# Odd heads' scores with swapped token halves, in a recurrent attention with two feed-forward layers on one core

## The chip, the core and the metric

The program runs on one core of a Trainium2 chip: a matrix engine (TensorE, PE), a vector engine (DVE), a scalar engine (ACT), GpSimd (POOL) and SyncE (SP), which issues the DMAs here. Times are microseconds on the device for one execution; lower is better.

## What is computed

An attention with a decaying state, token by token, over 4 batch entries, 8 heads, 768 tokens, 48 columns per head, and behind it two feed-forward layers on 3072 tokens of width 384:

```python
for t in range(S):
    cur = np.einsum('bhd,bhe->bhde', u[None] * kt, vt)
    y[:, :, t] = np.einsum('bhd,bhde->bhe', rt, state + cur)
    state = wt[:, :, :, None] * state + np.einsum('bhd,bhe->bhde', kt, vt)
# x: y with the heads side by side
xn = x / rms * rms_g
x = (silu(xn @ w_gate) * (xn @ w_val)) @ w_out         # d_ff 1536
out = (s * np.maximum(x @ w_in, 0) ** 2 + b) @ w_out2  # d_ff 2048
```

All of it is float32.

## The kernel before

Tokens are cut into 6 chunks of 128. A pair of chunk and batch entry is a block `jb` (24 of them, four to a chunk); `attention(jb, t)` does one. Both feed-forward layers take a chunk at a time, all four batch entries side by side, so that a dense pass on PE streams 512 columns: L646 is the product into the hidden width, L629 to L631 the product out of it (three passes for each of three output tiles, since a number is split into a high and a low part). The attention of a chunk runs while the first layer of the chunk before it is on PE.

Nothing is issued in the order of the code. Each step is handed to a planner (`op`) with a due time `t`, a cost for each engine that can do it, and what it reads and writes. The planner plays the program through with these costs, takes on each engine the ready step that is due first, and writes every engine's instructions in that order. A hundred or so due times are set by hand in a table, by the number of the operation, up to number 921. Waits between engines follow from what is read and written. The planner's costs that the prediction uses, in us: a dense pass 0.226; ACT's copy of one bank 0.19 + 0.65e-3 x 512 = 0.523; a select 0.60; the way from a step's end to a step on another engine 0.20 after PE, 0.15 after ACT and 0.10 after POOL; a DMA issue at least 0.47.

A block from the 13th (`jb` 12) on goes like this. SP loads decays (`w`), `r` and `k` of a block turned so that head columns lie on partitions (even heads on partitions 0 to 47, odd on 64 to 111, four head pairs `h` side by side), the natural `r` and `k` (`n`), and `v` with tokens on partitions. DVE scans the decays into products; `r` and `k` are multiplied with them (DVE or POOL). `k` is turned by a DVE transpose and a round trip through DRAM (`kd`, read back into `raw`, which the code calls TK). Then, on PE:

- **scores** (L404): for each head pair h, token half c0 and parity p, a product of 64 tokens of k with the tokens of r from c0 on. c0 = 0 gives 128 columns, c0 = 64 gives 64, since earlier tokens are masked. Its 64 results land on PSUM partitions c0 to c0 + 63, and its inputs lie on partitions from 64p on, so that each such product takes one of four quarters of the array. p chooses the PSUM bank.
- ACT copies each of the two banks to SBUF (128x512, `AT`), POOL sets what lies on or below the diagonal to zero (L426, affine_select, in place).
- **state** (L445) and **sums** (L454), one step for the planner: r with the carried state, and the masked scores with `v`, 64 output tokens at a time; then the products for the new state (L463), which read `v` and TK.
- DVE adds the term of u, ACT and POOL normalize, DVE transposes the result, and SP writes it to DRAM (`xt`) and, with the chunk's last block, reads it back for the layers.

SP issues its DMAs in the planner's order, each when what it waits for is there.

Of the kernel before, what the change touches and what calls it, by code (L numbers as in the profile page):

```python
# [17 lines left out]
ALU = mybir.AluOpType  # L18
# [4 lines left out]
B, H, S, D = 4, 8, 768, 48  # L23
C = 128
NC = S // C
HP = H // 2
DM = H * D
# [20 lines left out]
W_TINY, W_HUGE = 1.125 * 2.0 ** -15, 1.875 * 2.0 ** 16 - 2.0 ** -7  # L48
FA, HALF = 6, (4, 6)
ATT = 30.0, 6.0, 0.0, 18.0, 20.0, 20.0, 20.0, 0.0  # L50
TD, LATE = 3, 60
ORDER = -200, -190, -170, -160, -180, -150
FIRST_OPS = {
# [19 lines left out]
TURNED, EARLY, NU, NM, NZ, LENT = 12, 12, 4, 4, 8, 6  # L73
# [145 lines left out]
def mm(n, k=1):  # L219
    return k * (0.013 + n / 2400.0)  # L220
# [3 lines left out]
def body(ctx: ExitStack, tc: tile.TileContext, rkw, nat, w1, w2, cst, out):  # L224
    nc = tc.nc
# [5 lines left out]
    def tiles(n, name, shape, dt=F32):  # L231
        return [sb.tile(shape, dt, name=f"{name}{i}") for i in range(n)]
# [15 lines left out]
    OT = tiles(2, "o", [128, NB])  # L248
    IN = tiles(2, "in", [128, RKW])
    VT = tiles(2, "v", [128, H, D])  # L250
    NT, = tiles(1, "n", [128, 2, H, D])
    EB = [[t] for t in tiles(2, "eb", [RW, HP, WL])]
    KT = tiles(1, "kt", [128, HP, RW])
    AT = tiles(3, "a", [128, HP, C])
# [47 lines left out]
    def op(when, engines, fn, reads=(), writes=(), port=True):  # L302
        if planned[0]:
            reads, writes = [alias.get(k, k) for k in reads], [alias.get(k, k) for k in writes]
            plan.add(when, engines, fn, reads, writes, port)
        else:
            fn(next(iter(engines)))

    def dma(when, dst, src, nbytes, reads=(), writes=(), land=0.0):
        op(when, {"sp": max(0.47, nbytes / 350e3 + 0.06) + 0.5 * (when == -300)}, lambda e: nc.sync.dma_start(  # L310
            out=dst, in_=src), reads, writes, land)

    def tt(when, engines, n, dst, a, b, f, reads, writes):
        cost = {"dve": vec2(n), "pool": gps(n)}
        port = not any(k[0] == "ps" for k in reads)
        op(when, {e: cost[e] for e in engines}, lambda e: E[e].tensor_tensor(dst, a, b, f), reads, writes, port)  # L316

    def cp(when, n, dst, src, reads, writes, func=AF.Copy, **kw):
        op(when, {"act": act(n)}, lambda e: nc.scalar.activation(dst, src, func, **kw), reads, writes)  # L319
# [3 lines left out]
    def ring(name, of):  # L323
        rings[name] = rings.get(name, -1) + 1
        return of[rings[name] % len(of)]
# [9 lines left out]
    def attention(jb, t):  # L335
        q, b = jb % 2, jb % B
        AVK = [("av", q, h0) for h0 in range(0, H, 2)]
        ke, re, ne = (DVE, DVE, DVE) if jb < EARLY else (BOTH, BOTH, BOTH)
        last = jb >= NJ - B
        a, v, g, z = IN[q][:RW], VT[q], RG[q], q if jb < NZ else 0  # L340
        n = [RK[z][:, i * DM:(i + 1) * DM].rearrange("p (h d) -> p h d", h=H) for i in range(2)]
        ET, BT, kt, xg = EB[0][z], EB[1][z], KT[z], XG[z]
        ek, bk, nk, tk, xk = ("E", z), ("bk", z), ("n", z), [("kt", z)], ("xg", z)
        turned = jb >= TURNED
        rk = RK[z][:RW, 0:HP * C].rearrange("p (h t) -> p h t", h=HP)
        r = a[:, OR:OK].rearrange("p (h t) -> p h t", h=HP)
        k = a[:, OK:].rearrange("p (h t) -> p h t", h=HP)
        if jb in (TURNED, TURNED + 1):
            op(t - 15, {"pool": 0.5}, lambda e: nc.gpsimd.memset(IN[q][96:128, OK:], 0.0), (), [("k", q)], False)
        tl = [FIRST[jb] + 0.1 * i for i in range(4)] if jb < B else [t - 14 + 0.1 * i for i in range(4)]  # L350
        dma(tl[0], a[:, 0:OR], rkw[jb, :, 0:OR], RW * OR * 4, (), [("w", q)])
        dma(tl[1], a[:, OR:], rkw[jb, :, OR:], RW * 2 * HP * C * 4, (), [("r", q), ("k", q)])
        if jb >= NU:
            dma(tl[2], RK[z], nat[jb, :, DM:], 128 * 2 * DM * 4, (), [nk])
        dma(tl[3], v.rearrange("p h d -> p (h d)"), nat[jb, :, 0:DM], 128 * DM * 4, (), [("v", q)])

        op(t, {"dve": 1.15}, lambda e: nc.vector.tensor_tensor_scan(
            ET.rearrange("p h t -> p (h t)"), a[:, 0:HP * WL], ones.rearrange("p h t -> p (h t)"), 0.0,
# [16 lines left out]
        if turned and not last:  # L375
            tk = [("kt", i) for i in range(4)]
# [3 lines left out]
        sc = [PS[i].rearrange("p (h t) -> p h t", h=HP) for i in i2]  # L380
# [17 lines left out]
        def scores(e):  # L398
            for h in range(HP):
                for c0 in (0, 64) if jb >= B else (0,):  # L400
                    cols = slice(c0, c0 + 64 if jb >= B else C)
                    for p in range(2):
                        rows = slice(64 * p, 64 * p + D)
                        nc.tensor.matmul(sc[p][cols, h, c0:], k[rows, h, cols], r[rows, h, c0:],  # L404
                                         start=True, stop=True, skip_group_check=True)
            if kp is not None:
                for h in range(HP):
                    nc.tensor.transpose(kp[:, h, :], k[:, h, :], ident[:RW, :RW])  # L408
# [11 lines left out]
        A = [ring("a", (0, 1, 2, 3) if jb < NZ else (0, 1, 2)) for p in range(2)]  # L420
        for p in range(2):
            if jb < NM:
                tt(t, DVE, HP * C, AT[A[p]], sc[p], mask, ALU.mult, [("ps", i2[p]), "m"], [("a", A[p])])
                continue
            cp(t, HP * C, AT[A[p]], sc[p], [("ps", i2[p])], [("a", A[p])])
            op(t, {"pool": 0.60}, lambda e, s=A[p]: nc.gpsimd.affine_select(  # L426
                out=AT[s], in_=AT[s], compare_op=ALU.is_gt, fill=0.0, base=0, pattern=[[0, HP], [1, C]],
                channel_multiplier=-1), (), [("a", A[p])])
        if kp is not None:
            cp(t, HP * RW, kt, kp, [("ps", i)], tk)  # L430
        if jb < NU:
# [4 lines left out]
        Y = [PS[i][:, 0:DM].rearrange("p (h d) -> p h d", h=H) for i in (iy * 2)[:2]]  # L436
# [3 lines left out]
        def state(e):  # L440
            for h in range(HP):
                for c0 in (0, 64):
                    for p in range(2):
                        rows = slice(64 * p, 64 * p + D)
                        nc.tensor.matmul(Y[p][c0:c0 + 64, 2 * h + p, :], r[rows, h, c0:c0 + 64], ST[b][rows, h, :],  # L445
                                         start=h == 0, stop=False, skip_group_check=True)

        def sums(e):
            if jb >= B:
                state(e)  # L450
            for j in range(H):
                h, p = divmod(j, 2)
                for c0 in (0, 64):
                    nc.tensor.matmul(Y[p][c0:c0 + 64, j, :], AT[A[p]][:, h, c0:c0 + 64], v[:, j, :],  # L454
                                     start=jb < B and j == 0, stop=j >= H - 2, skip_group_check=True)
            if U is not None and jb >= B:
                news(e)
# [18 lines left out]
        reads = [("a", s) for s in A]  # L476
        if jb < B:
            op(t, {"pe": 1.0}, sums, reads + [("v", q)], [("ps", i)])
            op(t, {"pe": 0.7}, more, AVK + ["cs"], [("ps", i)])
            op(t, {"pe": 0.6}, news, [("v", q)] + tk, [("ps", iu)])  # L480
            ys, yk = PS[i][:, 0:DM], ("ps", i)
        else:
            op(t, {"pe": 1.5 + 0.6 * (not last)}, sums,
               reads + [("r", q), ("v", q), ("st", b)] + tk * (not last),
               [("ps", i) for i in iy] + ([] if last else [("ps", iu)]))
            ys, yk = YS[q], ("ys", q)
            for p in range(2):
                y2, a2, s2 = [x.rearrange("p (h j d) -> p h j d", h=HP, j=2)[:, :, p] for x in (
                    PS[iy[p]][:, 0:DM], AV[q].rearrange("p h d -> p (h d)"), ys)]
                tt(t, DVE, HP * D, s2, y2, a2, ALU.add, [("ps", iy[p])] + AVK, [yk])  # L490
# [5 lines left out]
        if not last:  # L496
            st, pmb = ST[b], PM[q].to_broadcast([RW, HP, D])
# [346 lines left out]
    beg, parts, t = {}, [], T0  # L844
# [7 lines left out]
    for jb in range(NJ):  # L852
        c, b = divmod(jb, B)
        if c == 0:
            t = ready = ORDER[b]
        elif c == 1:
            t = ready = beg[1, 0] - 34 + 9 * b
        elif c == 2:
            t = beg[1, 1] - LAG + 10.5 * b
            ready = max(t, beg[1, 1] + 0.01)  # L860
        else:
            t = beg[c - 1, 0] + b * (F1 * step + ATT[4]) / B - LAG
# [4 lines left out]
    for n, (c, fs) in enumerate(parts):  # L867
# [4 lines left out]
        t = beg[c, int(fs[0] > 0)]  # L872
        for p in part:
            d = (len(fs) * step + ATT[n]) * p[3] / (B * len(fs))
            seq.append((t, d) + p + (p[1] == fs[0], p[1] == fs[-1], int(fs[0] > 0)))
            t += d
    for f in range(F1):
        if f < FA:
            t = ORDER[B + f] if f < 2 else T0 + (f - 2) * 5.5
        else:  # L880
            t = beg[0, 1] + (f - FA - 4) * 5.5
# [7 lines left out]
    last = beg[NC - 1, 0]  # L889
    later(last, hand_over, last)  # L890
    for f in range(F2):
        t = last + min(2 * f // 3 + 3.5, F1 + 0.6 * (f - 15)) * 27 * mm(NB)
        later(t, weights, 1, f, t, slots_of(1, f))
    for c in range(NC):
        t2 = T1 + c * d2
        x = c % 2
        later(t2 - 12, x2_in, t2 - 12, c, x)
        for f in range(F2):
            d, q = d2 / F2, (len(seq) + f) % 2
            for b0, nb in ((0, 2), (2, 2)) if c == NC - 1 and f == F2 - 1 else ((0, B),):  # L900
                t = t2 + (f + b0 / B) * d
# [17 lines left out]
    with tc.If(flag > 0):  # L919
# [11 lines left out]
        w, r, k, kv, sc = (a[:RW] for a in big[:5])  # L931
        uc = PM[0][:, 0, :]
        with tc.For_i(0, B, 1) as b:
            with tc.For_i(0, HP, 1) as h:
                for dst, o, wd in ((w, 0, WL), (r, OR, C), (k, OK, C)):
                    src = rkw[:, :, o:o + HP * wd].rearrange("(c b) p (h t) -> b h p c t", b=B, h=HP)
                    nc.sync.dma_start(out=dst.rearrange("p (c t) -> p c t", c=NC), in_=src[b, h][:, :, wd - C:])
                vs = vn[:, 0:NC * 2 * D].rearrange("p (c m) -> p c m", c=NC)
                nc.sync.dma_start(
                    out=vs, in_=nat[:, :, 0:DM].rearrange("(c b) t (h m) -> b h t c m", b=B, h=HP)[b, h]  # L940
# [28 lines left out]
                for i in range(2):  # L969
                    vec.tensor_copy(vT[:2 * D, i * HC:(i + 1) * HC], ya[i])  # L970
                nc.sync.dma_start(
                    out=xd.rearrange("(h m) c b t -> h b m c t", h=HP)[h, b],
                    in_=vT[:2 * D].rearrange("p (c t) -> p c t", c=NC),
                )
        with tc.For_i(0, NC, 1) as c:
            x = IN[0][:, 0:KD * NB].rearrange("p (k t) -> p k t", k=KD)
# [17 lines left out]
            for ph, nf in ((0, F1), (1, F2)):  # L994
                for f in range(nf):
                    sw = range(3 * (f % 2), 3 * (f % 2) + 3 - ph)
                    weights(ph, f, 0, sw, clamp=True)
                    q, t = f % 2, SG[f % 2]
# [37 lines left out]
```

## Time and profile before

| | us |
|---|---|
| three runs | 967.93, 967.55, 966.31 |
| median | 967.55 |
| profiled execution | 967.64 |
| its span, first to last instruction | 965.9 |

A page of the profile gives, for each engine, its busy time and share of the span, then the busy tenths in 40 slices of 24 us, and the chain of work that ended last, followed back from the last instruction. The views behind it list instructions in order of time, groups of instructions, and waits. The matrix engine's products are pipelined, so they overlap, and a busy time is the union of what ran. A float32 product of the attention shows as two passes.

### The profile page before, as it was taken

What the parts mean: (1) busy time and instruction counts of PE and PEld (TensorE: products, weight loads), DVE (VectorE), ACT (ScalarE), POOL (GpSimd) and SP (SyncE); (2) the same over time, 40 slices, a digit from 0 to 9 for tenths busy, and PEclk for the clock granted to TensorE, in tenths of its full rate; (3) what the DMA queues carried; (4) which work ended last, traced back from release to release, by engine and by line L of the source; (5) the groups of instructions that cost most, each with busy time, mean ns of one, the idle gap of its engine ahead of it and who ended that gap; (6) DMA issues with size and microseconds to landing.
All of it is one profiled execution on the core that took longest, in us unless ns stands there. A gap on an engine that the chain in (4) does not pass through costs nothing.

```text
span 965.9 us, 16522 instructions
## 1 busy us (share of the span) xinstructions
PE 952.9 (99%) x6585; PEld 788.7 (82%) x6589; DVE 635.2 (66%) x1051; ACT 378.8 (39%) x782; POOL 162.6 (17%) x211
## 2 busy tenths in 40 slices
PE   9999999999999999999999999999999999999996
PEld 5898998888888887888888878888888888888885
DVE  8999898547445445532588799987777874433332
ACT  4756545534323332332343353343433433433333
POOL 1212211255433323110025440000000000000000
PEclk9999999999999999999999999999999999999998
DMA  8655554245434443222466465553354530000001
GB/s 259 196 169 158 173 158 140 83 112 149 101 84 118 122 93 95 69 69 61 122 225 206 150 212 178 158 194 113 114 182 132 178 117 1 33 0 1 34 1 36
DMA packets 74422, 115.79 MB, mean 120 GB/s; under 512 B 28384, under 2 KB 48096, under 8 KB 74336
## 3 DMA queue, kind: packets, MB, share of 16 engines
q1 hardware_dynamic: 74336, 114.65, 39.6%
q8 instruction: 53, 0.87, 0.4%
q14 instruction: 33, 0.27, 0.1%
HBM read 99.16 MB, written 15.47 MB: 119 GB/s over the span
## 4 chain that ended last, share of the span: by engine, by line
PE 91%; DVE 5%; DMA 2%; ACT 1%; issue 1%; SPq 0%; POOL 0%; DVEq 0%
PE b L646 48%; PE b L629 12%; PE b L630 11%; PE b L631 11%; PE b L454 2%; PE b L404 2%; PE b L445 1%; DMA raw<-in_w 1%; DMA in<-in_rkw 1%; DVE pat L605 1%; DVE pat L603 1%; PE b L408 0%; PE b L822 0%; PE b L469 0%; DVE pat L599 0%
## 5 line engine op out<-in xcount | busy, mean ns | idle before, releaser
L646 PE MATMUL b<-xh,w 128*128 128x512 f32 (+1 forms) x1566 | 485.2, 374 | 0.9 <-DVE sg L316 0.6
L646 PEld LDWEIGHTS b<-xh,w 128*128 128x128 f32 x1566 | 287.7, 188 | 55.6 <-issue 1.9
L646 PE MATMUL b<-xl,w 128*128 128x512 f32 (+1 forms) x783 | 291.1, 372 | 0.0
L629 PE MATMUL b<-hh,w 128*128 128x512 f32 (+1 forms) x537 | 205.0, 382 | 1.1 <-ACT in L681 0.7
L630 PE MATMUL b<-hl,w 128*128 128x512 f32 (+1 forms) x537 | 202.5, 377 | 1.4 <-DVE hl L316 1.4
L631 PE MATMUL b<-hh,w 128*128 128x512 f32 (+1 forms) x537 | 202.1, 376 | 0.0
L319 ACT ACTIVATE sg<-b 128x512 f32<-128x512 f32 (+1 forms) x179 | 102.6, 573 | 249.1 <-PE b L646 245.0
L646 PEld LDWEIGHTS b<-xl,w 128*128 128x128 f32 x783 | 147.3, 188 | 25.4
L717 DVE SCALAR_TENSOR_TENSOR sg<-sg,cs,b 128x512 f32<-128x512 f32 (+1 forms) x97 | 71.9, 741 | 90.0 <-ACT sg L319 89.8
L630 PEld LDWEIGHTS b<-hl,w 128*128 128x128 f32 x537 | 101.0, 188 | 20.2 <-DVE hl L316 2.5
L629 PEld LDWEIGHTS b<-hh,w 128*128 128x128 f32 x537 | 101.0, 188 | 20.1 <-ACT in L681 0.9
L631 PEld LDWEIGHTS b<-hh,w 128*128 128x128 f32 x537 | 101.0, 188 | 18.5
L720 DVE SCALAR_TENSOR_TENSOR hl<-sg,cs,hh 128x512 fp32r<-128x512 f32 (+1 forms) x97 | 73.0, 753 | 43.4 <-ACT hh L319 43.2
L319 ACT ACTIVATE hh<-sg,cs 128x512 fp32r<-128x512 f32 (+1 forms) x97 | 70.1, 722 | 75.9 <-DVE sg L717 71.4
L319 ACT ACTIVATE hh<-sg 128x512 fp32r<-128x512 f32 (+1 forms) x82 | 47.6, 581 | 114.9 <-DVE sg L316 109.5
L316 DVE TENSOR_TENSOR sg<-b,sg 128x512 f32<-128x512 f32 (+1 forms) x82 | 51.0, 623 | 62.1 <-PE b L646 52.9
L316 DVE TENSOR_TENSOR hl<-sg,hh 128x512 fp32r<-128x512 f32 (+1 forms) x82 | 57.3, 698 | 18.2 <-ACT hh L319 17.5
L620 POOL TENSOR_TENSOR w<-pat,w 128x384 fp32r<-128x384 f32 x29 | 39.8, 1394 | 67.2 <-ACT w L610 67.2
L610 ACT ACTIVATE w<-pat 128x384 fp32r<-128x384 f32 x68 | 32.8, 520 | 37.5 <-DVE pat L605 37.3
L316 DVE TENSOR_TENSOR ys<-b,av 128x192 f32<-128x192 f32 x40 | 13.8, 351 | 47.8 <-PE b L454 47.8
L426 POOL TENSOR_SCALAR_AFFINE_SELECT a<-a 128x512 f32<-128x512 f32 x38 | 29.6, 796 | 85.7 <-ACT a L319 85.4
L603 DVE SCALAR_TENSOR_TENSOR pat<-raw,pat 128x768 uint32<-128x768 uint32 (+1 forms) x40 | 35.7, 894 | 0.0
(128 smaller groups left out, 843.4 us busy)
## 6 DMA issues: line engine op xcount, KB each, us to landing
raw<-in_w SPq DMA_DIRECT2D x56, 768.0 KB, 4.4
in<-in_rkw SPq DMA_DIRECT2D x24, 448.0 KB, 4.6
raw<-in_w SPq DMA_DIRECT2D x24, 384.0 KB, 3.6
n<-in_nat SPq DMA_DIRECT2D x18, 384.0 KB, 3.4
in<-in_rkw SPq DMA_DIRECT2D x24, 226.6 KB, 3.0
x2d<-o SPq DMA_DIRECT2D x21, 256.0 KB, 2.4
a<-in_rkw SPq DMA_DIRECT2D x24, 224.0 KB, 2.9
v<-in_nat SPq DMA_DIRECT2D x24, 192.0 KB, 4.0
```

The lines of the kernel that those rows point to most:

```text
L316: op(when, {e: cost[e] for e in engines}, lambda e: E[e].tensor_tensor(dst, a, b, f), reads, writes, port)
L319: op(when, {"act": act(n)}, lambda e: nc.scalar.activation(dst, src, func, **kw), reads, writes)
L426: op(t, {"pool": 0.60}, lambda e, s=A[p]: nc.gpsimd.affine_select(out=AT[s], in_=AT[s], compare_op=ALU.is_gt, fill=0.0, base=0, pattern=[[ ...
L603: op(t, {"dve": vec2(N)}, lambda e, word=word, pat=pat: nc.vector.scalar_tensor_tensor(pat(), word(1), 0xC0000000, pat(), ALU.bitwise_and, ...
L610: op(t, {"act": act(DM)}, lambda e, c=c, s=s, pat=pat: nc.scalar.activation(W[s][:, 0], pat(c).bitcast(F32), AF.Copy), [("pat", pi)], [("w ...
L620: op(t, {"dve": vec2(DM)} if ph == 0 else {"dve": vec2(DM), "pool": gps(DM)}, lambda e, c=c, s=s, pat=pat: E[e].tensor_tensor(W[s][:, 1], ...
L629: nc.tensor.matmul(dst, wt[:, 0, cols], xh, start=first, stop=False, skip_group_check=True)
L630: nc.tensor.matmul(dst, wt[:, 0, cols], xl, start=False, stop=False, skip_group_check=True)
L631: nc.tensor.matmul(dst, wt[:, 1, cols], xh, start=False, stop=last, skip_group_check=True)
L646: nc.tensor.matmul(dst, W[s][:, w, kk * 128:(kk + 1) * 128], xx[x][:, kk, sl], start=first and j == kk == 0, stop=last and kk == KD - 1 an ...
L717: op(t, {"dve": vec2(n)}, lambda e: nc.vector.scalar_tensor_tensor(sg, sg, s_col, p, ALU.mult, ALU.mult), [("ps", i)], [("sg", q)], False)
L720: op(t, {"dve": vec2(n)}, lambda e: nc.vector.scalar_tensor_tensor(hl, sg, b_col, hh.bitcast(F32), ALU.add, ALU.subtract), [("sg", q), ("h ...
```

## The change

From block 12 on, for the odd head pairs (h = 1 and 3) the scores of the first 64 tokens land on partitions 64 to 127 and those of the last 64 on partitions 0 to 63. So the masked scores of these heads have their token halves swapped on the partitions. `v` must then be swapped alike for their sums: `VS` (two buffers) is a copy of the odd head pairs' columns of v with the halves swapped, loaded from DRAM by two more DMAs for each block. And the diagonal lies elsewhere: instead of one select on POOL for each parity there are three, one for the even head pairs, one for partitions 0 to 63 of the odd ones (shifted by 64), and one for the first 64 columns of partitions 64 to 127.

```diff
-TD, LATE = 3, 60
+TD, LATE, EVEN = 3, 60, 12
@@
+    VS = tiles(2, "vs", [128, HP, D])
@@
-        turned = jb >= TURNED
+        turned, even = jb >= TURNED, jb >= EVEN
@@
         dma(tl[3], v.rearrange("p h d -> p (h d)"), nat[jb, :, 0:DM], 128 * DM * 4, (), [("v", q)])
+        if even:
+            for z in (0, 64):
+                dma(tl[3], VS[q][z:z + 64].rearrange("p (g x) d -> p g (x d)", g=2),
+                    nat[jb, 64 - z:128 - z, 0:DM].rearrange("t (g o m) -> t g o m", g=2, o=2)[:, :, 1],
+                    64 * 4 * D * 4, (), [("vs", q, z)])
@@
                     cols = slice(c0, c0 + 64 if jb >= B else C)
+                    to = slice(64 - c0, C - c0) if even and h % 2 else cols
                     for p in range(2):
                         rows = slice(64 * p, 64 * p + D)
-                        nc.tensor.matmul(sc[p][cols, h, c0:], k[rows, h, cols], r[rows, h, c0:],
+                        nc.tensor.matmul(sc[p][to, h, c0:], k[rows, h, cols], r[rows, h, c0:],
                                          start=True, stop=True, skip_group_check=True)
@@
-            op(t, {"pool": 0.60}, lambda e, s=A[p]: nc.gpsimd.affine_select(
-                out=AT[s], in_=AT[s], compare_op=ALU.is_gt, fill=0.0, base=0, pattern=[[0, HP], [1, C]],
-                channel_multiplier=-1), (), [("a", A[p])])
+            def keep(t, what, cost, base, n):
+                op(t, {"pool": cost}, lambda e, what=what: nc.gpsimd.affine_select(
+                    out=what, in_=what, compare_op=ALU.is_gt, fill=0.0, base=base, pattern=[[0, n], [1, what.shape[-1]]],
+                    channel_multiplier=-1), (), [("a", A[p])])
+
+            if not even:
+                keep(t, AT[A[p]], 0.60, 0, HP)
+                continue
+            pairs = AT[A[p]].rearrange("p (g o) t -> p g o t", o=2)
+            keep(t, pairs[:, :, 0], 0.37, 0, 2)
+            keep(t, pairs[0:64, :, 1], 0.37, -64, 2)
+            keep(t, pairs[64:128, :, 1, 0:64], 0.25, 0, 2)
@@
-                    nc.tensor.matmul(Y[p][c0:c0 + 64, j, :], AT[A[p]][:, h, c0:c0 + 64], v[:, j, :],
+                    vj = VS[q][:, j // 4 * 2 + p] if even and h % 2 else v[:, j, :]
+                    nc.tensor.matmul(Y[p][c0:c0 + 64, j, :], AT[A[p]][:, h, c0:c0 + 64], vj,
@@
-               reads + [("r", q), ("v", q), ("st", b)] + tk * (not last),
+               reads + [("r", q), ("v", q), ("st", b)] + [("vs", q, z) for z in (0, 64)] * even + tk * (not last),
```

## Rows read from the trace of the kernel before

**Rows 1.** The page: busy time by engine, granted clock by slice, the last chain.

```profile
PE 952.9 (99%) x6585; PEld 788.7 (82%) x6589; DVE 635.2 (66%) x1051; ACT 378.8 (39%) x782; POOL 162.6 (17%) x211
PEclk9999999999999999999999999999999999999998
PE 91%; DVE 5%; DMA 2%; ACT 1%; issue 1%; SPq 0%; POOL 0%; DVEq 0%
```

**Rows 2.** Order of time, PE, one block: start us, us, instruction, its form, count.

```profile
262.52 0.39 PE L646 MATMUL b<-xh,w 128*128 128x512 f32 x1
262.83 1.10 PE L404 MATMUL b<-in 48*64 48x128 f32 x32
263.87 0.50 PE L646 MATMUL b<-xh,w 128*128 128x512 f32 x1
...
266.27 0.39 PE L630 MATMUL b<-hl,w 128*128 128x512 f32 x1
266.50 0.39 PE L631 MATMUL b<-hh,w 128*128 128x512 f32 x1
266.81 0.68 PE L445 MATMUL b<-st,in 48*64 48x48 f32 x32
267.43 1.14 PE L454 MATMUL b<-v,a 128*64 128x48 f32 x32
```

**Rows 3.** Groups by form, PE, 218 to 462 us: busy us, mean ns | idle.

```profile
L404 PE MATMUL b<-in 48*64 48x128 f32 x192 | 13.2, 275 | 0.0
...
L404 PE MATMUL b<-in 48*64 48x64 f32 x192 | 9.9, 235 | 0.0
L445 PE MATMUL b<-st,in 48*64 48x48 f32 x352 | 7.5, 222 | 0.0
```

**Rows 4.** Groups by form, PE, window 262.83 to 263.10, the scores' first.

```profile
L404 PE MATMUL b<-in 48*64 48x64 f32 x8 | 0.4, 230 | 0.0
L404 PE MATMUL b<-in 48*64 48x128 f32 x4 | 0.4, 295 | 0.0
```

**Rows 5.** Groups by form, PE, window 263.71 to 263.86, the scores' end.

```profile
L404 PE MATMUL b<-in 48*64 48x128 f32 x5 | 0.5, 268 | 0.0
```

**Rows 6.** Order of time, POOL and ACT, the same block: evictions and selects.

```profile
264.93 1.25 POOL L426 TENSOR_SCALAR_AFFINE_SELECT a<-a 128x512 f32<-128x512 f32 x2 [1.12 <-ACT a L319]
...
264.28 1.07 ACT L319 ACTIVATE a<-b 128x512 f32<-128x512 f32 x2
```

**Rows 7.** Selects on POOL: L426 from 218 us (min/median/max ns); L817 at the start.

```profile
L426 POOL TENSOR_SCALAR_AFFINE_SELECT a<-a x24: 629/636/1087, 220.6 to 463.0; 128x512 f32<-128x512 f32 x24
...
L817 POOL TENSOR_SCALAR_AFFINE_SELECT mk<-mk 128x128 f32<-128x128 f32 x1 | 0.3, 293 | 0.1
```

**Rows 8.** SP: issues in order of time; its waits from 218 us (total, times, longest).

```profile
335.82 2.02 SPq L310 DMA_DIRECT2D raw<-kd  x4
337.89 0.49 SPq L310 DMA_DIRECT2D in<-in_rkw  x1
338.43 0.43 SPq L310 DMA_DIRECT2D v<-in_nat  x1
340.08 1.76 SPq L310 DMA_DIRECT2D xt<-pat  x4
...
SPq L310 <- PE b L463: 48.8, 8, 8.5
```

**Rows 9.** The last chain in order of time, 356 to 370: start, us, what.

```profile
356.67 0.52 PE b L463 x16
...
357.64 1.75 SPq L310
...
360.53 4.75 DMA in<-in_rkw
...
365.35 1.71 POOL in L316
...
367.08 1.85 DVE eb L357
```

**Rows 10.** Order of time, PE, the end of that chain.

```profile
368.78 0.39 PE L629 MATMUL b<-hh,w 128*128 128x512 f32 x1
369.56 0.50 PE L630 MATMUL b<-hl,w 128*128 128x512 f32 x1 [0.40 <-DVE hl L316]
```

**Rows 11.** Stretches: length, busy us of PE, PEld, DVE, ACT, POOL; clock; DMA.

```profile
218.00:480.00 262.00, 261.60 (x2251) 212.54 (x2250) 126.32 (x193) 85.00 (x164) 72.93 (x99) 1.00 0.38 98
480.00:540.00 60.00, 60.00 (x266) 49.68 (x265) 52.65 (x69) 23.82 (x45) 23.87 (x17) 1.00 0.61 202
540.00:570.00 30.00, 28.45 (x123) 22.64 (x122) 24.93 (x30) 11.57 (x23) 12.17 (x10) 1.00 0.54 178
```

## The prediction

> **What bounds the kernel now.** I read the first page from the top. TensorE is busy for 952.9 of 965.9 us, its granted clock is in the top tenth in all but the last of the 40 slices, and the chain that ended last runs on PE for 91% of the span [rows 1]. So a microsecond of PE time is a microsecond of the kernel, as long as nothing makes PE wait instead. The change touches blocks 12 to 23, whose scores lie at 218 to 462 us; there are 192 long and 192 short score passes in that stretch, 16 and 16 in each of the 12 blocks [rows 3].
>
> One block, in order of time [rows 2]: PE leaves the MoE stream at 262.52, runs 32 score passes from 262.83 and is back in the stream at 263.87. A dense pass costs 0.23 us there (266.27 to 266.50), so the scores take 263.87 - 262.52 - 0.23 = 1.12 us of PE. Then come nine dense passes of L646 and three of L629 to L631, 2.95 us in all, then state (266.81) and sums (267.43). The other eleven blocks look like it.
>
> Inside the scores: each fp32 product shows as two passes, and each pass uses one quarter of the array, picked by the head's parity p (rows) and by the half of the output partitions (columns). In the code the first token half always goes to column half 0 and streams 128 columns, the second to column half 1 and streams 64. Per parity, one quarter gets 8 long passes and its neighbour 8 short ones. At 263.10, 8 short and 4 long passes have started [rows 4]; in the window 263.71 to 263.86 only long ones run [rows 5]. Over the blocks the long passes cover 13.2/12 = 1.10 us and the short ones 9.9/12 = 0.83 us [rows 3]. The short quarters are done early, and the long quarters set the end.
>
> **Scores with the halves swapped for heads 1 and 3.** Each quarter then has 4 long and 4 short passes. Pitch of a long pass: 8 in a row cover 1.10 us with the last one 0.27 us long [rows 3, 5], so (1.10 - 0.27)/7 = 0.119 us. Pitch of a short one: the trace has no quarter that streams 64 columns undisturbed; the nearest are the 32 state passes (48 columns, 8 to a quarter) with 0.68 us, the last 0.22 us long [rows 2, 3], so (0.68 - 0.22)/7 = 0.066 us, and half a long pitch, 0.060. Four long passes become short: 4 x (0.119 - 0.066) = 0.21 us; with 0.060 it is 0.24. Against it stands that a quarter may wait once for its neighbour, one short pitch: 0.21 - 0.066 = 0.15. I take 0.20, close to the full value, since short passes start well ahead of earlier long ones [rows 4]. **12 x 0.20 = 2.4 us off PE; ends 1.8 and 2.9.**
>
> The quarters do run ahead: for each head the code issues 4 long and then 4 short passes, so of the first 12 in its order 8 are long, yet 8 of the first 12 to start are short [rows 4]. A rule speaks against that and against the gain. The Trainium skill ("TensorE: Matmul & The Clock Gate", Part 3, The mechanism) says that matmuls start and end strictly in program order. By that rule a block would gain nothing (first rival); the trace doesn't agree with it.
>
> **Sums.** The same 32 passes with the same shapes; for heads 1 and 3 the streamed operand is VS instead of v. Nothing on PE.
>
> **Three selects for one, on POOL.** Today two selects of 128x512 follow the two evictions, 264.93 to 266.18 [rows 6]; a median one takes 636 ns, the slowest of 24 took 1087, and the one 128x128 select took 293 [rows 7]. A line through 293 and 636 gives 408 ns for 256 elements per partition. New cost for one p: 408 + 408 + 293 = 1109 ns, for both 2.22 us instead of 1.27, and the last ends at 264.93 + 2.22 = 267.15. With one contention as in the slowest row, 0.45 us more, 267.60. If a small select costs what a large one does, 6 x 0.636 = 3.82 and the end is 268.75. I take 2.22, as the 128x128 row shows that the time falls with the size. Sums start at 267.43, so even in today's order 0.28 us of cover are left, where now it is 1.25.
>
> But the planner moves sums. In its own costs sums are ready 0.20 + 0.523 + 0.15 + 2 x 0.60 + 0.10 = 2.17 us after the scores, and PE is free after 2.04 (nine dense passes) + 0.68 (three) = 2.72. With 0.99 for each p it is 2.95, too late for 2.72, so three more dense passes go first and sums stand 0.68 us later. By the trace that is 267.43 + 0.68 = 268.11, 0.96 us after the estimated end of the selects. **Nothing on PE**, and the cover is gone once the six selects take 3.2 us.
>
> **What hangs on later sums.** The turned k of a later block is read back into the buffer that the new-state products free. In one place that chain is tight [rows 9]: the products end at 357.19, SP issues the read-backs (one takes 1.75 us), then the load of r and k at 360.53, which lands 4.75 us later; POOL's product and the scan on DVE to 368.9 follow, and hl comes late, so that PE goes from 368.78 to 369.56 [rows 10], 0.55 us over 0.23. With sums 0.68 later this wait grows to 1.23 us. If the 1.75 us don't recur (the four read-backs of the block before took 2.02 in all [rows 8], these 3.3), the chain is 1.3 shorter, and the wait is gone. Ends +0.68 and -0.55; I take 0, the middle. Its neighbours have no such wait.
>
> **Two more loads on SP for each block**, of 64 x 192 floats, in pieces of 384 bytes. An issue takes 0.4 to 0.5 us [rows 8], so about 0.9 us for each block and 11 in all, right after v. Behind them stand the writes of x (xt). In the block of [rows 8], v is issued by 338.86 and xt follows at 340.08, so the gap of 1.2 us covers them; SP waited 48.8 us for L463 alone in these blocks. Where there is no gap, xt is 0.9 us later, and xt is needed a chunk later. VS, like v, has two buffers, is freed by the sums two blocks earlier, and so is loaded more than a block ahead. **Nothing**, at most +0.9 once where a chunk's last x is awaited. Two tiles of 768 bytes per partition are added to SBUF; no buffer is taken away. The hand-set due times go up to operation 921, and the first operation of block 12 comes after that by my count of the planner's list, so none slides to another operation.
>
> **The sum.** 967.64 (the profiled execution: span 965.9 and 1.7 around it; the median is 967.55) - 2.4 + 0 = **965.2 us**, with -2.9 - 0.55 = 964.2 and -1.8 + 0.68 + 0.9 = 967.4 as ends.
>
> **Rivals.**
> *Quarters in lockstep* (the change doesn't do what it says). If passes started strictly in order, two heads would cost 4 x 0.119 = 0.476 us now and 2 x 0.119 + 4 x 0.066 = 0.502 after: a quarter that turns from short to long holds up its neighbour. That is +0.05 for each block, 12 x 0.05 = 0.6, **968.2 us**. Against it: [rows 4]. Nothing in the rows speaks for it but that a long quarter alone would look the same in either case, as it runs without a gap. 5%. (This is how the Trainium skill's rule above, from "TensorE: Matmul & The Clock Gate", would come out here.)
>
> *The gain is given back by new waits*. Everything after block 12 is planned anew, with 0.78 us more POOL and 0.94 more SP in each block's plan, and what stands behind a late step on DVE or SP is late too, as hl was behind the scan [rows 9]. Waits of PE like the 0.55 us above, or like the 1.55 us idle at 540 to 570 us where weights are prepared [rows 11], appear in other places. One to four of 0.55 more: **965.8 to 967.4 us**, 966.6 in the middle. For it: DVE is busy 52.65 of 60 us just before that stretch [rows 11]. Against it: PE idles 0.4 us in all from 218 to 540 [rows 11], and most late steps hang on PE itself, so they move with it. 25%.
>
> *POOL's selects end behind sums*, and the kernel is slower. Place: sums' wait for the last select. With the order planned above the wait begins once six selects take 3.2 us, and each 0.1 us beyond costs 12 x 0.1 = 1.2 us. At 636 ns each, 3.82 us, the wait is 0.64 us, 12 x 0.64 = 7.7: 967.64 - 2.4 + 7.7 = **972.9 us**. It is slower than before from 3.4 us on, 0.57 us for each select. For it: one select took 1087 ns [rows 7]. Against it: 293 ns for the small one [rows 7]. 10%.
>
> **How the numbers follow.** Forecast 60%, lockstep 5%, new waits 25%, selects 10%. About 0.2%, 1.9 us, is what a measurement can tell from no change, and the forecast of -2.4 lies close to it: I put nine tenths of its 60 with faster (0.54) and the rest with same; of new waits 0.02 faster, 0.21 same, 0.02 slower; lockstep is same; selects slower, 0.08, and 0.02 same. Faster 0.56, same 0.34, slower 0.10. The range runs from 963.9 (a shade below the low end, for a wait at 540 to 570 us that shortens) to 967.5 and leaves out lockstep, selects and some 0.05 more.
>
> **What would show it.** In the profile after: the step from the last dense pass before the scores to the first one after falls from 1.35 to about 1.15 us, long passes start in both column halves, and the busy time of long and of short passes draws together. Selects: 24 of 128x256 near 0.41 us, 24 of 64x256, 24 of 64x128 near 0.29, the last ending before sums start, and sums behind six passes of L629 to L631 instead of three. The place of 368.78 shows whether the wait grew. I am wrong if the step stays at 1.35 (quarters), if the step from state to sums, now 0.61, grows (selects), or if the steps shrink by 0.2 and the time doesn't (waits elsewhere).

## The result, and the profile after

The changed kernel takes **978.41 us** (median of 6), the kernel before 967.59 (median of 6 beside it): ratio 1.0111, interval 1.0095 to 1.0127, so 10.8 us slower. 965.2 was forecast, with a range up to 967.5, and a chance of 0.10 for slower. The profiled execution took 977.83 us with a span of 976.1.

The first page of after says little: PE is busy for 98% and the last chain runs mostly on it, as in [rows 1]. One slice of the granted clock has an 8.

```profile
PE 958.2 (98%) x6603; PEld 791.2 (81%) x6603; DVE 635.2 (65%) x1052; ACT 380.4 (39%) x785; POOL 181.3 (19%) x255
PEclk9999989999999999999999999999999999999999
PE 88%; DVE 5%; DMA 3%; ACT 1%; issue 1%; SPq 1%; POOL 1%; DVEq 0%; POOLq 0%; ACTq 0%
```

The scores did what was forecast. Order of time on PE in one block of after (start, us, instruction, form, count), beside [rows 2]: the step from the last dense pass to the next one is 253.66 - 252.51 = 1.15 us, where it was 1.35.

```profile
252.51 0.39 PE L648 MATMUL b<-hh,w 128*128 128x512 f32 x1
252.83 0.90 PE L411 MATMUL b<-in 48*64 48x128 f32 x32
253.66 0.50 PE L663 MATMUL b<-xh,w 128*128 128x512 f32 x1
...
257.64 0.39 PE L648 MATMUL b<-hh,w 128*128 128x512 f32 x1
257.96 0.68 PE L461 MATMUL b<-st,in 48*64 48x48 f32 x32
258.57 0.44 PE L471 MATMUL b<-v,a 128*64 128x48 f32 x8
```

In the groups by form over blocks 12 to 23 (busy us, mean ns), long and short passes now cover 10.8/12 = 0.90 and 10.5/12 = 0.88 us for each block, where [rows 3] had 1.10 and 0.83:

```profile
L411 PE MATMUL b<-in 48*64 48x128 f32 x192 | 10.8, 276 | 0.0
...
L411 PE MATMUL b<-in 48*64 48x64 f32 x192 | 10.5, 223 | 0.0
```

So where are the 10.8 us? A mark that stands in both traces tells it: the scores of block 12 start at 218.53 before and at 229.34 after, those of block 23 at 460.30 and 471.03. **All of it is lost ahead of the first block that the change touches**, and from one mark to the other the gain of the scores doesn't show either: 241.77 us before, 241.69 after. First before, then after, order of time on PE:

```profile
218.53 1.10 PE L404 MATMUL b<-in 48*64 48x128 f32 x32
...
460.30 1.10 PE L404 MATMUL b<-in 48*64 48x128 f32 x32
```

```profile
229.34 0.90 PE L411 MATMUL b<-in 48*64 48x128 f32 x32
...
471.03 0.90 PE L411 MATMUL b<-in 48*64 48x128 f32 x32
```

At the very start, SP has new work. Its issues in order of time, before:

```profile
2.20 0.90 SPq L310 DMA_DIRECT2D in<-in_rkw  x2
3.15 0.91 SPq L310 DMA_DIRECT2D cs<-in_cst  x2
4.10 0.53 SPq L310 DMA_DIRECT2D v<-in_nat  x1
4.68 1.03 SPq L310 DMA_DIRECT2D raw<-in_w  x2
```

and after:

```profile
2.21 0.89 SPq L311 DMA_DIRECT2D in<-in_rkw  x2
3.14 0.43 SPq L311 DMA_DIRECT2D cs<-in_cst  x1
3.62 2.83 SPq L311 DMA_DIRECT2D vs<-in_nat  x4
6.84 0.35 SPq L311 DMA_DIRECT2D cs<-in_cst  x1
7.74 0.33 SPq L311 DMA_DIRECT2D v<-in_nat  x1
```

The four loads of VS for blocks 12 and 13 go at 3.6 us, some 200 us early. VS is a new tile: for these two blocks nothing has used it before, so the loads wait for nothing. Their due times in the planner's list are 199.0 and 222.3; that of the second load of constants, behind them, is set by hand to 281.6. The planner gives SP what is ready and due first.

From there the first 220 us are in another order, with the same products. PE lacks work in places, and where it does, the planner has it run filler passes on zeros. Up to block 12 there are 75 of them, where the trace before shows 57 and 61 loads of their weights (some records of matmuls are missing), so 14 more. Groups by form, before and after:

```profile
L822 PE MATMUL b<-zero 128*128 128x512 bf16 x42 | 12.3, 428 | 0.3 <-issue 0.2
L822 PE MATMUL b<-zero 128*128 128x256 bf16 x15 | 3.2, 278 | 0.0
```

```profile
L839 PE MATMUL b<-zero 128*128 128x512 bf16 x52 | 15.4, 430 | 0.0
L839 PE MATMUL b<-zero 128*128 128x256 bf16 x23 | 3.5, 274 | 0.6 <-DVE sg L317 0.6
```

It waits more too. Stretches from the start to block 12's scores, before and after (length, busy us of PE, PEld, DVE, ACT, POOL; clock; DMA), have 3.86 and 7.00 us in which PE isn't busy:

```profile
0.00:218.53 218.53, 214.67 (x2222) 182.28 (x2226) 179.23 (x347) 115.26 (x325) 49.85 (x83) 1.00 0.54 161
0.00:229.34 229.34, 222.34 (x2241) 186.13 (x2241) 179.12 (x344) 116.40 (x327) 58.52 (x84) 0.99 0.53 154
```

In shorter stretches of after, PE is busy for 1.50 and 0.93 of 2 us at 118 to 122, and the granted clock falls to 0.50, its lower level (1.2 GHz), up to about 129:

```profile
118.00:120.00 2.00, 1.50 (x13) 1.30 (x11) 1.68 (x3) 1.77 (x6) 0.92 (x2) 1.00 0.54 114
120.00:122.00 2.00, 0.93 (x4) 0.49 (x4) 1.73 (x3) 1.33 (x4) 0.21 (x2) 1.00 0.82 281
122.00:124.00 2.00, 1.59 (x7) 1.59 (x8) 2.00 (x6) 0.52 (x1) 0.07 (x1) 0.54 0.25 101
124.00:126.00 2.00, 2.00 (x35) 1.76 (x33) 2.00 (x4) 0.38 (x1) 0.00 (x0) 0.50 0.65 197
126.00:128.00 2.00, 2.00 (x12) 1.68 (x9) 2.00 (x5) 1.52 (x3) 0.88 (x2) 0.50 0.47 119
128.00:130.00 2.00, 2.00 (x46) 1.79 (x47) 1.38 (x2) 0.42 (x1) 0.85 (x2) 0.75 0.02 5
```

The clock's part is 2 x (0.46 + 0.50 + 0.50 + 0.25) = 3.4 us of work that full speed would have done. The fillers' busy time grew by 18.9 - 15.5 = 3.4 us too, and PE's idle time by 7.00 - 3.86 = 3.1. Together that is 9.9 of the 10.8 us; the remaining 0.9 is in the busy time of the other products, and its cause isn't shown.

### The profile page after: what moved, and what is told of

It reads as the page before. It is cut to its first block, busy times and chain, and to the rows that moved or that the text cites. A ratio compares the mean times of both kernels' runs of the same rounds, so it can differ in the third digit from the quotient of the medians.

```text
span 976.1 us, 16636 instructions
## 1 busy us (share of the span) xinstructions
PE 958.2 (98%) x6603; PEld 791.2 (81%) x6603; DVE 635.2 (65%) x1052; ACT 380.4 (39%) x785; POOL 181.3 (19%) x255
## 4 chain that ended last, share of the span: by engine, by line
PE 88%; DVE 5%; DMA 3%; ACT 1%; issue 1%; SPq 1%; POOL 1%; DVEq 0%; POOLq 0%; ACTq 0%
PE b L663 47%; PE b L646 11%; PE b L647 11%; PE b L648 11%; PE b L471 2%; PE b L411 2%; PE b L461 1%; DMA raw<-in_w 1%; SPq L311 1%; DMA in<-in_rkw 1%; DVE pat L622 1%; POOL a L434 0%; PE b L486 0%; DMA v<-in_nat 0%; DVE pat L620 0%
## 5 line engine op out<-in xcount | busy, mean ns | idle before, releaser
L317 DVE TENSOR_TENSOR hl<-sg,hh 128x512 fp32r<-128x512 f32 (+1 forms) x82 | 55.3, 675 | 16.0 <-ACT hh L320 15.3
L434 POOL TENSOR_SCALAR_AFFINE_SELECT a<-a 128x256 f32<-128x256 f32 (+3 forms) x86 | 46.3, 563 | 76.3 <-ACT a L320 74.6
```

The lines of the kernel that those rows point to most:

```text
L434: op(t, {"pool": cost}, lambda e, what=what: nc.gpsimd.affine_select(out=what, in_=what, compare_op=ALU.is_gt, fill=0.0, base=base, patter ...
```

## The experiments

**Loads of VS held behind v.** The changed kernel, but a load of VS is planned to wait for the load of v of its block:

```diff
-                    64 * 4 * D * 4, (), [("vs", q, z)])
+                    64 * 4 * D * 4, [("v", q)], [("vs", q, z)])
```

> The changed kernel, with each load of VS planned behind the load of v of its block, so that no load of VS is free to go at the start. The planner's order up to block 12 is then that of the kernel before on every engine. Theory A (the 10.8 us were lost ahead of block 12, because the four loads of VS for blocks 12 and 13 wait for nothing and came first on SP): block 12's scores start at about 218 us as before, the step around the scores is 0.92 us, and the time is 965 us (963.5 to 966.5), ratio 0.996 to 0.999. Theory B (the selects, the later sums or the SP issues of blocks 12 to 23 cost it): it stays at 975 to 979.

972.38 us (968.72 to 974.16), ratio 1.0051 (1.0037 to 1.0064). The profiled execution was the fastest, 968.72. In it block 12's scores start at 218.61, as before. So theory A holds for what lies ahead of block 12. The list of steps is the same here as in the changed kernel, so the loss isn't a shift of the hand-set due times by the added steps. But 972 lies between the two expectations: the gain didn't come, and a second loss shows, which the early one had covered. Waits of PE from 218 to 480 us (total, times, longest), against the single one of [rows 10]:

```profile
PE b L663 <- DVE sg L317: 2.9, 2, 1.9
PE b L647 <- DVE hl L317: 0.7, 1, 0.7
```

The last chain, in order of time, leads to the longest of them. It is the chain of [rows 9] in another block: the products for the new state end at 227.65, SP reads the turned k back, then r and k are loaded and land 5.4 us later, DVE's next operation needs them, and sg, behind it on DVE, comes late.

```profile
227.14 0.52 PE b L480 x16
227.65 0.35 SPq L311
...
228.65 1.36 SPq L311
...
230.61 5.42 DMA in<-in_rkw
...
237.85 0.69 DVE sg L317
...
238.58 1.45 PE b L663 x5
```

**The four loads alone.** The kernel before plus the two loads of VS for blocks 12 and 13 each, which nothing reads:

```diff
+        if jb in (12, 13):
+            for z in (0, 64):
+                dma(tl[3], VS[q][z:z + 64]..., nat[jb, 64 - z:128 - z, 0:DM]..., 64 * 4 * D * 4, (), [("vs", q, z)])
```

> The kernel before, with nothing but the four loads of VS for blocks 12 and 13 added, planned as in the change (nothing reads them). Theory A: the whole loss and none of the gain, 967.6 + 10.8 + 0 to 2.4, so 978 to 981 us, with block 12's scores at about 229 us. Theory B: 967.6.

978.54 us, ratio 1.0107 (1.0092 to 1.0123). Four loads of 48 KB whose data nobody reads make the whole loss.

**The loads issued, but not planned.** The order of before on every engine; inside the step of the constants SP first issues the four loads:

```diff
+        def constants(e):
+            for jb in (12, 13):
+                for z in (0, 64):
+                    nc.sync.dma_start(out=VS[jb % 2][z:z + 64]..., in_=nat[jb, 64 - z:128 - z, 0:DM]...)
+            nc.sync.dma_start(out=cs[:, 0:CU], in_=cst[:, 0:CU])
+
-        dma(CONST, cs[:, 0:CU], cst[:, 0:CU], 128 * CU * 4, (), ["cs"])
+        op(CONST, {"sp": max(0.47, 128 * CU * 4 / 350e3 + 0.06)}, constants, (), ["cs"], 0.0)
```

> The kernel before in exactly its order on every engine, with the same four loads issued by SP just ahead of the constants, without the planner knowing of them. Theory A1 (it is the 2 to 3 us of SP itself, ahead of the constants and first inputs, that delay the start): most of the loss, 974 to 980 us. Theory A2 (it is the planner's new order of the first 220 us, to which the hand-set due times no longer fit): 968 to 971 us.

970.54 us, ratio 1.0026 (1.0016 to 1.0036). Issued early in the old order, the loads cost 2.7 us by the medians; SP takes 2.67 us to issue them in this trace.

**The loads planned, but not issued.** The order of the kernel with the four loads; their steps issue nothing, and the step of v issues them in blocks 12 and 13:

```diff
+        if jb in (12, 13):
+            for z in (0, 64):
+                op(tl[3], {"sp": 0.47}, lambda e: None, (), [("vs", q, z)], 0.0)
```

> The other half: the planner is told of the four loads at the start, as in the kernel with only these loads, so that the order of all else is the same as there, but SP issues them only behind v of blocks 12 and 13. Theory A1: 967 to 970 us. Theory A2: 976 to 980 us.

978.64 us, ratio 1.0113 (1.0098 to 1.0129). Theory A2: **the loss is the order**. SP does nothing more than before at the start, and the time is that of the kernel with the loads. The two halves don't add up: 10.8 here and 2.7 for the early issue, against 10.7 for both together. So in the new order the early issue adds nothing that shows.

**All of the work in the order of before.** VS is loaded inside the step of v, the three selects are one step of 0.60; every engine has the order of before.

```diff
@@
-            keep(t, pairs[:, :, 0], 0.37, 0, 2)
-            keep(t, pairs[0:64, :, 1], 0.37, -64, 2)
-            keep(t, pairs[64:128, :, 1, 0:64], 0.25, 0, 2)
+            def select(e, s=A[p]):
...
+                keep(pairs[:, :, 0], 0, 2)
+                keep(pairs[0:64, :, 1], -64, 2)
+                keep(pairs[64:128, :, 1, 0:64], 0, 2)
+
+            op(t, {"pool": 0.60}, select, (), [("a", A[p])])
```

> All of the change's work, but with nothing of it told to the planner: the two loads of VS are issued inside the step of v, the three selects inside one step of 0.60. Every engine then has exactly the order of the kernel before. Theory C (the change's work itself is a gain of 2.4 us, and what was lost comes from the planner's new order alone): 965.3 us, ratio 0.996 to 0.999, step around the scores 0.92 us over a dense pass, and sums without a wait of more than 0.1 us. Theory D (the longer selects and the SP issues cost on the chip, whatever the order): 968 to 972.

966.25 us beside 968.54 of before, ratio 0.9986 (0.9966 to 1.0005). The loss of 10.8 us is gone, but by the interval this can't be told from the kernel before. Of the 2.4 us some are missing. In the trace, sums of two blocks wait pass by pass for selects, 0.72 and 0.39 us over the usual 0.97. The worst, order of time on PE:

```profile
289.87 0.68 PE L476 MATMUL b<-v,a 128*64 128x48 f32 x8
290.38 0.29 PE L476 MATMUL b<-vs,a 128*64 128x48 f32 x4
290.94 0.32 PE L476 MATMUL b<-vs,a 128*64 128x48 f32 x4 [0.27 <-POOL a L437]
```

and on POOL, where two products of natural r and k end only at 288.6, after the evictions:

```profile
286.05 1.01 POOL L317 TENSOR_TENSOR n<-n 128x384 f32<-128x384 f32 x1 [3.48 <-DMA n<-in_nat]
287.13 1.49 POOL L317 TENSOR_TENSOR n<-n,cs 128x384 f32<-128x384 f32 x1
288.58 2.31 POOL L437 TENSOR_SCALAR_AFFINE_SELECT a<-a 128x256 f32<-128x256 f32 x6
```

**One of the two planned.** First the loads of VS as steps behind v, with the selects as one step of 0.60; then the loads inside the step of v, with the selects as three steps.

> As the kernel with the order of before, but the loads of VS are steps of their own, planned behind v; the selects stay one step of 0.60. PE, DVE, ACT and POOL keep the order of before, SP's own order changes. Theory C1 (the waits behind block 12 come from the selects' planned time, which puts sums three dense passes later): as the kernel with the order of before, 965 to 966.5. Theory C2 (they come from SP's order): 969 to 973, as with all of it planned and the loads held behind v.

966.95 us, ratio 0.9992 (0.9973 to 1.0011). The loads as steps of their own cost nothing that these runs show, so theory C2 is out.

> The opposite: the loads of VS stay inside the step of v, the selects are three planned steps of 0.37, 0.37 and 0.25, so that sums stand three dense passes later in the blocks from 12 on. Theory C1: 969 to 973, with waits of PE behind late loads of r and k at about 236, 328 and 371 us. Theory C2: 965 to 966.5.

971.43 us, ratio 1.0021 (1.0003 to 1.0038), beside the same runs of before. By the medians that is 5.2 and 4.5 us over the two kernels with the selects as one step. PE waits in its trace (218 to 480 us) as in the kernel with the loads held:

```profile
PE b L665 <- DVE sg L317: 3.0, 3, 1.9
PE b L649 <- DVE hl L317: 1.7, 2, 1.4
```

From block 12's scores to block 23's its trace has 245.18 us, the kernel with all of the work in the order of before 240.53. Theory C1: the second loss comes from how the selects are planned, as three steps of 0.99 for one of 0.60; that the time and not the number of steps does it wasn't tried by itself. That it goes by way of later sums is read from the traces: in block 13 state starts 5.14 us behind the start of scores, 1.37 us more than in the order of before, and ahead of four of the five waits, all but one of 0.17 us, DVE has waited 2.1 to 3.7 us for a load of r and k to land.

**The scores alone.** The order of before, no VS, one select:

```diff
+                    to = slice(64 - c0, C - c0) if jb >= 12 and h % 2 else cols
...
-                        nc.tensor.matmul(sc[p][cols, h, c0:], k[rows, h, cols], r[rows, h, c0:],
+                        nc.tensor.matmul(sc[p][to, h, c0:], k[rows, h, cols], r[rows, h, c0:],
```

> The kernel before in its order, with the odd heads' score passes of blocks 12 to 23 sent to the swapped halves and nothing else: no loads of VS, one select as before, so that the odd heads' sums of these blocks leave out the swap back and mask in the wrong place. It measures the saving on PE by itself. By the step around the scores (1.12 to 0.92 us, 12 blocks): 2.4 us less than before, 965.3 to 966 us, ratio 0.9975. If quarters balanced this way gave nothing to the time: 967.6 to 968.5.

965.24 us beside 968.12, ratio **0.9973 (0.9964 to 0.9982)**, 1.7 to 3.5 us less by the interval. Order of time on PE, blocks 12 and 23: 239.51 us from one to the other, where before had 241.77; 11 blocks at 0.2 are 2.2.

```profile
218.55 0.90 PE L405 MATMUL b<-in 48*64 48x128 f32 x32
...
458.06 0.90 PE L405 MATMUL b<-in 48*64 48x128 f32 x32
```

**All of the work in the order of before, once more**, beside the scores alone.

> The same kernel as the one with all of the change's work in the order of before, once more, beside the scores alone. If selects and loads cost nothing: the same time as the scores alone. If sums wait for the selects where POOL is late, as in two blocks of the first trace (0.73 and 0.35 us): about 1 us more than the scores alone, 1.4 less than before, ratio 0.9985.

966.76 us, ratio 0.9992 (0.9981 to 1.0003): 1.5 us over the scores alone by the medians, and again not to be told from the kernel before. What the complete change adds to the scores (loads, longer selects, sums that read VS) takes back half of the gain or more even where no order changes; which of the three does it these two runs don't tell.

**Even head pairs first.** As that kernel; POOL selects the even head pairs of both parities first, and sums take them first (the edit of sums is shown).

```diff
-            for j in range(H):
+            heads = (0, 1, 4, 5, 2, 3, 6, 7) if even else range(H)
+            for j in heads:
```

> All of the change's work in the order of before, with two orders inside steps turned: POOL selects the even head pairs of both parities first and then the odd ones, and sums take the even head pairs first. Theory (what the complete change lacks against the scores alone is sums waiting pass by pass for late selects, 0.6 to 1.1 us in a trace): these waits go, sums take 0.97 us in every block, 965.2 to 965.8 us, ratio 0.997 to 0.998. If the missing microsecond comes from the loads or from POOL taking time from DVE: 966.3 to 967, as without the turn.

966.97 us beside 967.82, ratio 0.9985 (0.9972 to 0.9997). It can't be told from the kernel without the turn. In its trace sums of two blocks still wait, 0.13 and 0.36 us, so the waits shrank but didn't go, and the theory that they make the whole difference to the scores alone isn't borne out. The trace of the same work without the turn, beside that of the scores alone, says where to look. It spans 2.6 us more (965.5 and 962.9). From block 12's scores to block 23's it takes 0.83 more (240.34 and 239.51). From 540 to 600 us, behind all blocks, PE idles 3.09 us where the scores alone have 1.07 and the kernel before 1.55. With even heads first it is 1.08, so this part doesn't come with the complete change every time; what the rest is stays open.

## Why the prediction was wrong, point by point

**What bounds the kernel**: right for the stretch of the change, and read too narrowly. I asked what the change adds in blocks 12 to 23 and took the first 218 us as given.

**Scores**: right. 0.20 us for each block was forecast and is in the trace of after (1.15 for 1.35); the scores alone give 2.6 us by the ratio, 2.4 forecast. Passes do not keep to one order over the quarters; with strict order the step would have grown, by the sum of the first rival, and it fell by 0.20. The rule of the Trainium skill ("TensorE: Matmul & The Clock Gate", Part 3, The mechanism) is the other way, and the traces don't agree with it: of the first 12 passes to start 8 are short [rows 4], where the order of the code has 4.

**Two more loads on SP: the step that failed.** "VS, like v, has two buffers, is freed by the sums two blocks earlier, and so is loaded more than a block ahead. Nothing, at most +0.9 once where a chunk's last x is awaited." That is true from block 14 on. For blocks 12 and 13 v is held by blocks 10 and 11, but VS by nobody. The last sentence there, that no hand-set due time slides to another operation, was true and beside the point: the table fits one plan, and the four steps changed that plan. I had the numbers: the due times stand in the planner's list beside the 281.6 of the constants. It cost 10.7 us (the four loads alone), and the two runs that split issue from plan show that the order makes it. Which of the steps put elsewhere is worst isn't told apart by them.

**Later sums: the mechanism was right, the size wrong.** I had 0.68 us for each block. Blocks 18 to 23 have just that: from the start of scores to the start of state there are 4.45 us in after and 3.98 before, with scores 0.20 shorter. Blocks 12 to 17 have some 1.35 us or more. In the block shown above state begins 4.30 us after the scores (257.96 - 253.66), where [rows 2] had 2.94, and nine dense passes of the second product stand ahead of it instead of three: 1.36 us later. I took the chain over the read-backs and r and k in the one place where it showed, and gave 0 for it with +0.68 as an end; "its neighbours have no such wait" was true of the trace before and said nothing of sums that come later. With sums later PE waits in three places (3.6 us, loads held) and in five (4.7 us, selects planned), in all but the shortest of them after DVE waited for r and k; the whole chain is shown only for the longest. By the medians the planned selects cost 4.5 to 5.2 us. The changed kernel has two such waits, 2.1 us.

**Selects**: a single one sized right, the cover mis-sized. 408, 408 and 293 ns were forecast. Over the 24 of each shape in after the medians are 408, 402 and 293; some take longer, up to 1329 ns, so that the means are 513, 458 and 303:

```profile
L434 POOL TENSOR_SCALAR_AFFINE_SELECT a<-a 128x256 f32<-128x256 f32 x24 | 12.0, 513 | 48.6 <-ACT a L320 48.3
L434 POOL TENSOR_SCALAR_AFFINE_SELECT a<-a 64x256 f32<-64x256 f32 x24 | 10.6, 458 | 0.1
L434 POOL TENSOR_SCALAR_AFFINE_SELECT a<-a 64x128 f32<-64x128 f32 x24 | 6.8, 303 | 0.9
```

"So even in today's order 0.28 us of cover are left" started them at the evictions, as in the block of [rows 6]. Where POOL is in its products of n by then, they start 1 us later, and sums wait: 1.1 us in all in the first trace with the order of before. In the changed kernel itself later sums hide them, as forecast; it was the planned, longer time that paid for the cover.

**The rivals.** Lockstep fell with the scores. New waits, at 25% and up to 967.4, was the right kind, but I let it begin at block 12 and sized it from one wait. The select rival was not what made it slower.

**The sum.** The parts don't simply add up: -2.6 (scores), about +5 (selects planned) and +10.7 (four loads) are 13, and 10.8 was measured. In the traces, the stretch from block 12 to block 23 takes 241.77 us before, 241.69 after and 243.52 with the loads held, so PE's order of these blocks, the same in the last two, costs less where they start late: PE waits 2.1 us there in after and 3.6 with the loads held.

And the kernel with the loads held was 3.7 us slower in the median than in its profiled execution. How executions of one order can differ by that much is in another trace. The profiled execution of the kernel with even head pairs first is the longest of its 13, 971.03 us. Its order up to block 12 is that of before, yet block 12's scores start at 223.57, 5.0 us later. At 6 to 10 us PE is busy for 2.57 of 4 us (before: 3.46), and from about 11 to 21 us the granted clock is at its lower level, which costs 2 x (0.24 + 4 x 0.50 + 0.32) = 5.1 us:

```profile
8.00:10.00 2.00, 1.16 (x16) 0.97 (x16) 2.00 (x3) 0.00 (x0) 0.41 (x2) 1.00 1.08 416
10.00:12.00 2.00, 1.98 (x13) 1.95 (x15) 2.00 (x5) 0.31 (x1) 0.21 (x1) 0.76 0.99 316
```

With the loads held, three of the four executions without a profile have a mean granted clock of 0.994 to 0.996 where the profiled one has 0.999, which is some 3 to 5 us of 970; the fourth has 0.999 and is 2.9 us slower all the same, and that stays open.

## What to carry to other kernels

A step that depends on nothing is free at time zero: for each buffer that a change adds, ask what holds its first uses, not what holds the later ones, and give it a dependence if the answer is nothing. Where a planner or a table tuned by hand sets the order, a change's first effect is the new order, on every engine and ahead of the code that it touches; put the change into the old order first, measure it there, and only then tell the planner. And a passing mark in both traces, such as the start of one block's scores, tells in a minute on which side of it the time was lost.

## What the hardware showed that I had not expected

A select over 64 partitions costs about what one over 128 does: 293 ns in the median for 64x128 beside 293 for 128x128 [rows 7], and 402 for 64x256 beside 408 for 128x256. The granted clock fell to half behind 4 us in which PE was busy for 2.4, and stayed there for about 7 us, in most of which PE was busy again; the Trainium skill ("TensorE: Matmul & The Clock Gate", Part 1) has that PE's clock is gated down after idling, and the trace agrees, though PE had products between gaps of 1.00, 0.46 and 0.52 us. At the start of the execution of 971.03 us it fell to half behind 4 us in which PE was busy for 2.57, and stayed there for about 10 us, in the order of before. And short passes that are evened out over the quarters hardly wait for each other: 0.20 us saved in a block (1.35 to 1.15), where the full exchange of four long passes for four short ones was estimated, from the pitches of the trace before, at 0.21.
